# Linear attention and a mixer MLP, gated: tails in two DMAs, the gate vector from GpSimd, an earlier x tile, and four small moves of order

## The chip, the cores and the metric

The kernel runs on one core of a Trainium2 chip. A core has TensorE (PE, with its weight loads shown apart as PEld), VectorE (DVE), ScalarE (ACT), GpSimd (POOL) and SyncE (SP), and 16 DMA engines that move data between HBM and the on-chip memory. The metric is the device time of one execution in microseconds (us). Before the change its median over 3 runs is 1114.06 us (1113.56 to 1114.44).

## The reference

One input x of 2048 tokens by 576 features goes through two blocks, and a gate mixes the results. Everything is float32.

```
g   = sigmoid(sum(x * gate_w))                    # one number per token
# block A: linear attention, 32 heads of 18 features
q, k, v = split(x @ wqkv)
phi(t)  = where(t > 0, t + 1, exp(t)) + 1e-6
kv  = sum over tokens of phi(k) v^T               # 18 x 18 for each head
z   = sum over tokens of phi(k)
o   = (phi(q) kv) / (phi(q) z + 1e-6)
a   = o @ wo
# block B: layer norm, 576 -> 4608, gelu, 4608 -> 576
y   = (x - mean) / sqrt(var + 1e-5)
b   = gelu(y @ w1 + b1) @ w2 + b2
out = g * a + (1 - g) * b
```

## The kernel before, in words

**Tiles.** The tokens stand in 16 tiles of 128. The 576 features of a contraction are four blocks of 128 and a *tail* of 64. A float32 operand is cut into a high part (an fp32r copy made by ACT) and a low part (DVE subtracts the copy from the original), and a product is the sum of high x high, high x low and low x high. For a tail, high and low part share one block: rows 0 to 63 hold the high part, rows 64 to 127 the low one. So the tail of an x tile or of a weight is loaded twice, into both halves of the partitions. `load_twice` (L137) does that in one DMA whose source has an outer dimension of 2 with stride 0:

```
by.dma_start(dst, bass.AP(tensor=src.tensor, offset=src.offset, ap=[[0, 2], [ld, r], [st, n]]))
```

In the trace `t<-in_xm` is the main part of an x tile (256 KB) and `t<-in_xe` its tail (64 KB); `s<-in_wm` and `s<-in_we` are those of a half of the key or query weights (576 and 144 KB); `wv<-in_wve` is the tail of the value weights (288 KB). `y<-t` and `y<-s` are the cuts of an x tile and of a weight, on ACT (copy) and on DVE (subtraction). All helper calls are recorded with line L113, so that groups are told by their tiles.

**Order.** Every engine runs its instructions in the order in which the Python program calls them (the class `InOrder`, L105), so a wait holds all that stands behind it on its engine. All loads and stores are issued by SP, but for four of the first weight, which ACT issues. SP and ACT share eight completion semaphores for their DMAs in rotation: a DMA is issued only when the one eight places ahead of it has landed. The gate vector (`accs<-in_gw`, 2.4 KB) is loaded by two DMAs from SP.

**First stage (L481 to L566).** Three x tiles and four weight halves are loaded and cut. `first_keys(n, half)` is the product of 14 matmuls of x tile n with a half of the key weights; the order list gives pairs of blocks of x and of w, where 0 to 3 are high main blocks, 5 to 8 low main blocks, and 4 and 9 the tails. Between the first and the second product PE turns the gate vector into a column (five transposes), which DVE copies behind the second key half as its column 289, so that the gate's sum comes out of the key product; a column of ones behind it gives the mean.

**Loop over the other 13 tiles (L640 to L662).** Step n computes keys of tile n (28 matmuls), cuts tile n + 1, applies phi, adds the products of tile n - 1 to the sums over tokens (`ps<-ks,xs`), and, but for the last three tiles, computes queries (28 matmuls). Tiles live in a ring of three buffers (`yt`). Beside this, jobs in a table by step (`at(n, f)`) prepare the MLP's input: a *pair* of tiles is loaded (`accs<-in_xm`, `accs<-in_xe`, and its means and scales `accs<-moments`), normalised on DVE (`accs<-accs`), combined and stored as `yd`. `scale_in` and `scale_out` make 1/sqrt(var) of a pair: a power on POOL and one Newton step of four tiny DVE operations; `share_moments` transposes the small table (four DVE transposes) and stores it.

**Attention out (L892 to L906).** In step i of the second loop PE transposes the queries of tile i + 1 (`transpose_q`; ACT and DVE cut the result into `qt`), multiplies tile i's by the values (`attend`, 28 matmuls `ps<-wp,qt`), DVE divides the queries of tile i + 3 by their sums (`normalize`: reduce, add, reciprocal, multiply) and POOL multiplies those of tile i + 4 by the sums (`weigh`).

**MLP (L1163 on).** 18 windows of 14 products each with a seven-product scheme, with jobs in a list sorted by a number `14 * w + x`; `split_w1(k, False)` and `split_w1_rest(k, False)` cut the second part of first-layer weight chunk k into `wb`.

Of the kernel before, what the change touches and what calls it, by code (L numbers as in the profile page):

```python
# [17 lines left out]
P = 128  # L18
S, D, H, DH, F = 2048, 576, 32, 18, 4608
NT = S // P  # L20
HALF = D // 2
# [95 lines left out]
def tile_gated_mix(ctx: ExitStack, tc: tile.TileContext, x, xm, xe, wm, we, wvm, wve, wo, um, ue, w2, b1, b2, gw, out):  # L117
# [19 lines left out]
    def load_twice(dst, src, by=sp):  # L137
        (ld, r), (st, n) = src.ap
        by.dma_start(dst, bass.AP(tensor=src.tensor, offset=src.offset, ap=[[0, 2], [ld, r], [st, n]]))
# [344 lines left out]
    load_w(KEY, 0, ((0, 1), (1, 2), (2, 4), (4, 5)), act)  # L484
    act.activation(tiny, ones[:, 0:1], AF.Exp)
    load_x(first[1])
    sp.dma_start(gwr[:, :D], gw.rearrange("(a n) -> a n", a=1))
    sp.dma_start(gwr[:, D:], gw[4 * P:D].rearrange("(a n) -> a n", a=1))
# [13 lines left out]
    split_w(KEY, 0, pieces=((0, 1), (1, 2)))  # L502
    split_x(first[0], ((4, 5),))
    split_w(KEY, 0, pieces=((2, 4), (4, 5)))

    def first_keys(n, half):
        project(first[n], KEY, half, HI_FIRST, 3 * half + n)
# [10 lines left out]
    first_keys(0, 0)  # L518
# [3 lines left out]
    first_keys(1, 0)  # L522
    split_x(first[2])
    first_keys(2, 0)
    dve.tensor_copy(wraw[KEY, 1][:, :, HALF:HALF + 1], column[:, :, None])
    dve.memset(wraw[KEY, 1][:, :, HALF + 1:HALF + 2], 1.0)
# [113 lines left out]
    for n in range(FIRST, NT):  # L640
        i, before = ORDER[n], ORDER[n - 1]
        if n + 2 < NT:
            load_x(ORDER[n + 2])
        project(i, KEY, 0)
        keys_phi(i, 0)
        project(i, KEY, 1)
        if n + 1 < NT:
            split_x(ORDER[n + 1])
        keys_phi(i, 1)
        moments_of(before)  # L650
        if n + 1 < NT:
            load_xn(ORDER[n + 1])
        keys_split(i)
        add_products(before, 0)
        split_xn(i)
        run(3 * n)
        if n < NT - LATE:
            projected(i, QUERY)
            queries_out(i)
        run(3 * n + 1)  # L660
        add_products(before, 1)
        run(3 * n + 2)  # L662
# [190 lines left out]
    def during(i, f, *args):  # L853
        extra[min(i, NT - 1)].append(lambda: f(*args))
# [25 lines left out]
    during(5, scale_out, NP - 1)  # L880
    during(5, share_moments, NP - 1)
# [10 lines left out]
    for i in range(NT):  # L892
# [7 lines left out]
        if i + 3 < NT:  # L900
            normalize(i + 3)
# [194 lines left out]
    for k in range(HALF_TIME):  # L1096
        w, x = k // 2, 7 * (k % 2)
        if k >= EARLY:
            x1 = x + (0, 0)[k % 2] if k + 1 < HALF_TIME else x - 1
# [151 lines left out]
```

## Time and profile before

| | |
|---|---|
| median of 3 runs | 1114.06 us |
| the profiled execution | 1112.49 us, of it 1110.7 us span |
| PE busy | 1091.2 us (98%) |
| DVE, ACT, POOL busy | 883.5, 571.5, 303.1 us |
| DMA | 206.21 MB, 186 GB/s on the mean |
| granted TensorE clock | 0.998 |

The span is cut by the program into the first stage (to about 47 us), the loop over tiles (to about 197 us), sums and value projection (to about 220 us), attention out (to about 290 us) and the MLP. A matmul's end in the trace is modelled, so a stretch in which PE is "busy" can hide waiting; the number of matmuls in a window tells it. Rows of the timeline give start, duration, engine, operation, tiles written and read, how many instructions were merged, and in brackets the idle time before and what ended it. SPq and ACTq are the issue of DMAs on SP and ACT.

### The profile page before, as it was taken

The page shows a single profiled execution, that of the slowest core. Times are in us where ns is not written, and L with a number is a line of the kernel's source. Part 1 is how long each engine was busy: PE and PEld are TensorE (multiplying, and loading weights), DVE is VectorE, ACT ScalarE, POOL GpSimd, SP SyncE. Part 2 cuts the span into 40 slices and gives each one's busy share as a digit, 9 for nine tenths or more (in the row PEclk, how much of TensorE's full clock was granted, in tenths as well). Part 3 has the DMA queues.
Part 4 walks back from the last instruction along what each step waited for, and adds up shares of the span by engine and source line. Part 5 has one row for each costly group of instructions (what it writes and reads, how often), then busy time and mean ns, then how long its engine had stood idle before and what let it go on. Part 6 is the DMA issues. An engine that isn't in the chain of part 4 may idle for free.

```text
span 1110.7 us, 17958 instructions
## 1 busy us (share of the span) xinstructions
PE 1091.2 (98%) x6657; PEld 997.7 (90%) x6657; DVE 883.5 (80%) x1296; ACT 571.5 (51%) x918; POOL 303.1 (27%) x216
## 2 busy tenths in 40 slices
PE   7999998999999999999999999999999999999998
PEld 7999997999878989889898899989999999999998
DVE  3699988699789999999999996895665656656687
ACT  3767656344566645555555554455444444444450
POOL 0000000672022222312232223333443424324300
PEclk9999999999999999999999999999999999999999
DMA  5385675584974537445465489646534434434342
GB/s 168 110 265 200 219 240 194 188 341 177 320 258 178 191 140 253 158 159 182 172 213 179 144 297 399 202 150 203 149 106 141 149 106 141 146 108 140 106 152 86
DMA packets 126342, 206.21 MB, mean 186 GB/s; under 512 B 9113, under 2 KB 82105, under 8 KB 122288
## 3 DMA queue, kind: packets, MB, share of 16 engines
q1 hardware_dynamic: 125566, 204.34, 54.8%
q8 instruction: 52, 0.85, 0.3%
q10 hardware_dynamic: 690, 0.74, 0.2%
q14 instruction: 34, 0.28, 0.1%
HBM read 135.95 MB, written 69.09 MB: 185 GB/s over the span
## 4 chain that ended last, share of the span: by engine, by line
PE 76%; DVE 12%; DMA 5%; ACT 3%; issue 2%; SPq 1%; ACTq 0%; DVEq 0%
PE ps L113 76%; DVE h L113 2%; DVE accs L113 2%; DMA s<-in_we 2%; DVE wa L113 2%; DVE w_ops L113 1%; DVE qz L113 1%; SPq L113 1%; DMA t<-in_xe 1%; ACT wa L113 1%; DVE u L113 1%; ACT e L113 1%; DMA w_raw<-in_ue 1%; DVE w2r L113 1%; DVE w_raw L113 1%
## 5 line engine op out<-in xcount | busy, mean ns | idle before, releaser
L113 PEld LDWEIGHTS ps<-w_ops,h 128*128 128x128 f32 x2856 | 427.1, 188 | 41.9 <-DVE w_ops L113 2.9
L113 PE MATMUL ps<-w_ops,h 128*128 128x288 f32 x2856 | 452.7, 295 | 1.7 <-ACT accs L113 0.9
L113 PE MATMUL ps<-y,wa 128*128 128x512 f32 x1008 | 277.0, 392 | 0.5 <-DVE wa L113 0.3
L113 POOL TENSOR_TENSOR u<-u 128x512 f32<-128x512 f32 x116 | 176.0, 1542 | 280.7 <-DVE h L113 149.0
L113 DVE TENSOR_TENSOR accs<-ps,accs 128x576 f32<-128x576 f32 x210 | 158.5, 755 | 106.6 <-PE ps L113 99.7
L113 PE MATMUL ps<-y,wb 128*128 128x512 f32 x756 | 202.4, 393 | 0.1
L113 PEld LDWEIGHTS ps<-y,wa 128*128 128x128 f32 x1008 | 174.1, 188 | 20.9 <-DVE wa L113 0.8
L113 ACT ACTIVATE u<-u,b1s 128x512 f32<-128x512 f32 x110 | 79.8, 725 | 215.6 <-DVE u L113 215.6
L113 PE MATMUL ps<-y 128*128 128x288 f32 (+1 forms) x1088 | 157.1, 303 | 9.8 <-ACT y L113 6.1
L113 PEld LDWEIGHTS ps<-y 128*128 128x128 f32 x1088 | 152.5, 194 | 14.0 <-ACT y L113 7.4
L113 DVE TENSOR_TENSOR h<-u,h 128x1024 fp32r<-128x1024 f32 x119 | 157.2, 1321 | 3.5 <-ACT h L113 3.5
L113 PEld LDWEIGHTS ps<-y,wb 128*128 128x128 f32 x756 | 132.4, 188 | 18.7 <-DVE u L113 0.7
L113 ACT ACTIVATE h<-u 128x1024 fp32r<-128x1024 f32 x119 | 125.2, 1053 | 39.0 <-PE ps L113 36.8
L113 POOL TENSOR_TENSOR w2r<-w2r 128x576 f32<-128x576 f32 x48 | 73.0, 1521 | 258.3 <-DVE w2r L113 149.4
L113 ACT ACTIVATE u<-ps 128x512 f32<-128x512 f32 x110 | 65.1, 594 | 101.7 <-PE ps L113 101.6
L113 DVE TENSOR_TENSOR u<-ps,u 128x512 f32<-128x512 f32 x110 | 75.4, 686 | 36.4 <-PE ps L113 23.4
L113 DVE TENSOR_TENSOR w_ops<-w2r,w_ops 128x576 fp32r<-128x576 f32 x119 | 98.1, 825 | 0.0
L113 ACT ACTIVATE w_ops<-w2r 128x576 fp32r<-128x576 f32 x119 | 79.7, 670 | 0.5 <-DMA w2r<-in_w 0.5
L113 PE MATMUL ps<-wp,qt 128*128 128x288 f32 x448 | 63.3, 297 | 2.0 <-DVE qt L113 2.0
L113 PEld LDWEIGHTS ps<-wp,qt 128*128 128x128 f32 x448 | 59.9, 188 | 2.3 <-DVE qt L113 2.3
L113 DVE TENSOR_TENSOR accs<-accs 128x384 f32<-128x384 f32 (+3 forms) x67 | 58.4, 881 | 2.3 <-DMA accs<-moments 0.8
L113 DVE TENSOR_TENSOR w_raw<-w_raw 128x384 f32<-128x384 f32 x64 | 53.8, 841 | 1.6 <-DMA w_raw<-in_ue 0.8
(139 smaller groups left out, 843.0 us busy)
## 6 DMA issues: line engine op xcount, KB each, us to landing
wa<-w1d SPq DMA_DIRECT2D x80, 320.0 KB
w2r<-in_w SPq DMA_DIRECT2D x72, 288.0 KB
w1d<-wa SPq DMA_DIRECT2D x16, 1280.0 KB
wb<-w1d SPq DMA_DIRECT2D x60, 320.0 KB
y<-yd SPq DMA_DIRECT2D x14, 1280.0 KB
w1d<-wb SPq DMA_DIRECT2D x16, 960.0 KB
w_raw<-in_um SPq DMA_DIRECT2D x96, 128.0 KB
yd<-ys SPq DMA_DIRECT2D x15, 640.0 KB
```

What stands on the lines that cost most here:

```text
L113: return lambda *args, **kwargs: self.tc.keep_in_program_order(op(*args, **kwargs))
```

## The change

Seven edits; the arithmetic stays the same, but for the order in which the first product is summed.

- `load_twice` issues two DMAs of 64 partitions each, both from the same source, where it issued one of 128. It is called for 16 x tiles, four weight halves and the value weights: 21 more DMAs.
- The two DMAs of the gate vector are issued by GpSimd (ahead of its mask) and no longer by SP.
- ACT issues the tail of the first key half behind its table load and the `tiny` activation, and no longer ahead of them.
- The first product's order is the high and low blocks 0 and 1, then 2 and 3, then the products with the weight's low part, and the two with the tails last. ACT and DVE cut weight blocks 2 and 3 ahead of the x tile's tail.
- The column of the gate vector is copied ahead of the cut of the third x tile.
- From step FIRST on, the load in the loop is for tile n + 3 and stands behind the cut of tile n + 1; it was for n + 2 at the head of the step. In the first of these steps both are issued.
- The Newton step and the transposes of the last pair stand inside `normalize` of attention step 5, ahead of its multiply; they stood at the end of the step. The cut of `wb` for chunk 2 stands half a place later.

```diff
     def load_twice(dst, src, by=sp):
-        (ld, r), (st, n) = src.ap
-        by.dma_start(dst, bass.AP(tensor=src.tensor, offset=src.offset, ap=[[0, 2], [ld, r], [st, n]]))
+        for half in range(2):
+            by.dma_start(dst[half * 64:(half + 1) * 64], src)
...
     load_x(first[0])
-    load_w(KEY, 0, ((0, 1), (1, 2), (2, 4), (4, 5)), act)
+    load_w(KEY, 0, ((0, 1), (1, 2), (2, 4)), act)
     act.activation(tiny, ones[:, 0:1], AF.Exp)
+    load_w(KEY, 0, ((4, 5),), act)
+    pool.dma_start(gwr[:, :D], gw.rearrange("(a n) -> a n", a=1))
+    pool.dma_start(gwr[:, D:], gw[4 * P:D].rearrange("(a n) -> a n", a=1))
     load_x(first[1])
-    sp.dma_start(gwr[:, :D], gw.rearrange("(a n) -> a n", a=1))
-    sp.dma_start(gwr[:, D:], gw[4 * P:D].rearrange("(a n) -> a n", a=1))
     load_x(first[2])
...
     split_x(first[0], ((0, 4),))
-    split_w(KEY, 0, pieces=((0, 1), (1, 2)))
+    split_w(KEY, 0, pieces=((0, 1), (1, 2), (2, 4)))
     split_x(first[0], ((4, 5),))
-    split_w(KEY, 0, pieces=((2, 4), (4, 5)))
-
-    def first_keys(n, half):
-        project(first[n], KEY, half, HI_FIRST, 3 * half + n)
+    split_w(KEY, 0, pieces=((4, 5),))
+
+    def first_keys(n, half, order=HI_FIRST):
+        project(first[n], KEY, half, order, 3 * half + n)
...
-    first_keys(0, 0)
+    first_keys(0, 0, HH[:2] + LH[:2] + HH[2:] + LH[2:] + HL + TAIL)
     split_x(first[1])
...
     first_keys(1, 0)
+    dve.tensor_copy(wraw[KEY, 1][:, :, HALF:HALF + 1], column[:, :, None])
+    dve.memset(wraw[KEY, 1][:, :, HALF + 1:HALF + 2], 1.0)
     split_x(first[2])
     first_keys(2, 0)
-    dve.tensor_copy(wraw[KEY, 1][:, :, HALF:HALF + 1], column[:, :, None])
-    dve.memset(wraw[KEY, 1][:, :, HALF + 1:HALF + 2], 1.0)
...
     for n in range(FIRST, NT):
         i, before = ORDER[n], ORDER[n - 1]
-        if n + 2 < NT:
+        if n == FIRST:
             load_x(ORDER[n + 2])
...
         if n + 1 < NT:
             split_x(ORDER[n + 1])
+        if n + 3 < NT:
+            load_x(ORDER[n + 3])
         keys_phi(i, 1)
...
-    during(5, scale_out, NP - 1)
-    during(5, share_moments, NP - 1)
...
         if i + 3 < NT:
-            normalize(i + 3)
+            normalize(i + 3, (0,))
+            if i == 5:
+                scale_out(NP - 1)
+                share_moments(NP - 1)
+            normalize(i + 3, (1,))
...
-            x1 = x + (0, 0)[k % 2] if k + 1 < HALF_TIME else x - 1
+            x1 = x + 0.5 * (k == EARLY) if k + 1 < HALF_TIME else x - 1
```

Three places show what the table of instructions makes of it. The first is ACT at the start of the program; `s` is the first key half, `t` the first x tile, `y` their cuts:

```order
 L113 DMA s<-in_wm 128x288 x2
 L113 DMA s<-in_wm 128x2x288
-L113 DMA s<-in_we 128x1x288
 L113 ACT_TABLE_LOAD
 L113 ACTIVATE tiny<-ones 128x1
+L113 DMA s<-in_we 64x288 x2
 L113 ACTIVATE y<-t 128x512
 L113 ACTIVATE y<-s 128x288 x2
+L113 ACTIVATE y<-s 128x576
 L113 ACTIVATE y<-t 128x128
-L113 ACTIVATE y<-s 128x576
 L113 ACTIVATE y<-s 128x288
```

The tail's DMA went behind the table load and became two; the cut of weight blocks 2 and 3 (`128x576`) went ahead of that of the x tail.

The second is SP in steps 12 and 13 of the tile loop, first as it was (`yd` are stores of prepared pairs, `xn` the x tile in its other layout):

```order
L113 DMA t<-in_xm 128x512
L113 DMA t<-in_xe 128x1x128
L113 DMA xn<-in_x 128x576
L113 DMA accs<-in_xm 128x2x256
L113 DMA accs<-in_xe 128x1x128 x2
L113 DMA accs<-in_xm 128x2x256
L113 DMA accs<-in_xe 128x1x128 x2
L113 DMA accs<-moments_107 128x512
L113 DMA yd_131<-ys_545 128x2x640
L113 DMA t<-in_xm 128x512
L113 DMA t<-in_xe 128x1x128
L113 DMA xn<-in_x 128x576
```

and now:

```order
L113 DMA t<-in_xm 128x512
L113 DMA t<-in_xe 64x128 x2
L113 DMA xn<-in_x 128x576
L113 DMA accs<-in_xm 128x2x256
L113 DMA accs<-in_xe 128x1x128 x2
L113 DMA accs<-in_xm 128x2x256
L113 DMA accs<-in_xe 128x1x128 x2
L113 DMA accs<-moments_107 128x512
L113 DMA yd_131<-ys_554 128x2x640
L113 DMA xn<-in_x 128x576
```

The x tile stands at the same place of SP's queue, but it is the last of the 16 where it was the last but one, and the place behind the pair's loads, where the last tile stood, is empty.

The third is DVE in attention step 5 (`qz` are the sums of queries, `mt`, `mr` and `mrt` the moments), before:

```order
L113 RECIPROCAL qz<-qz 128x32
L113 SCALAR_TENSOR_TENSOR acc_right<-acc_right,qz 128x576
L113 TENSOR_TENSOR mt<-mr 128x2
L113 TENSOR_TENSOR mt<-mt 128x2
L113 TENSOR_SCALAR mt<-mt 128x2
L113 TENSOR_TENSOR mr<-mr,mt 128x2
L113 STREAM_TRANSPOSE mrt<-mr 32x32 x4
L113 TENSOR_TENSOR qt<-ps,qt 128x512
```

and now:

```order
L113 RECIPROCAL qz<-qz 128x32
L113 TENSOR_TENSOR mt<-mr 128x2
L113 TENSOR_TENSOR mt<-mt 128x2
L113 TENSOR_SCALAR mt<-mt 128x2
L113 TENSOR_TENSOR mr<-mr,mt 128x2
L113 STREAM_TRANSPOSE mrt<-mr 32x32 x4
L113 SCALAR_TENSOR_TENSOR acc_right<-acc_right,qz 128x576
L113 TENSOR_TENSOR qt<-ps,qt 128x512
```

The eight small operations went ahead of the multiply that ends `normalize`.

## The prediction

> **What bounds the kernel now.** I read the shares of the engines first, then PE's waits, then the timeline and the counts of matmuls in short windows around each wait.
>
> ```profile
> PE 1091.2 (98%) x6657; PEld 997.7 (90%) x6657; DVE 883.5 (80%) x1296; ACT 571.5 (51%) x918; POOL 303.1 (27%) x216
> ...
> PE ps L113 <- ACT y L113: 6.1, 4, 3.4
> PE ps L113 <- DVE k L113: 3.4, 1, 3.4
> PE ps L113 <- DVE qt L113: 2.0, 1, 2.0
> ```
>
> PE sets the end. What an edit is worth is the time by which PE gets earlier to work it then does without a gap. Its three named waits lie where the change works: the cuts `y` of the start (four waits), phi of the keys near the loop's end, `qt` in the attention.
>
> The start first, by the timeline of PE, ACT and ACT's queue:
>
> ```profile
> 2.22 1.12 ACTq L113 DMA_DIRECT2D s<-in_we  x1
> 4.77 0.61 ACT L113 ACTIVATE y<-t 128x512 fp32r<-128x512 f32 x1
> 5.29 0.76 ACT L113 ACTIVATE y<-s 128x288 fp32r<-128x288 f32 x2
> 5.77 0.94 PE L113 MATMUL ps<-y 128*128 128x288 f32 x2 [0.45 <-ACT y L113]
> 7.29 0.31 ACT L113 ACTIVATE y<-t 128x128 fp32r<-128x128 f32 x1 [1.23 <-DMA t<-in_xe]
> 7.50 0.67 ACT L113 ACTIVATE y<-s 128x576 fp32r<-128x576 f32 x1
> 8.22 1.81 PE L113 MATMUL ps<-y 128*128 128x288 f32 x6 [1.51 <-ACT y L113]
> 12.92 0.44 ACT L113 ACTIVATE y<-s 128x288 fp32r<-128x288 f32 x1 [4.75 <-DMA s<-in_we]
> 13.41 2.06 PE L113 MATMUL ps<-y 128*128 128x288 f32 x6 [3.38 <-ACT y L113]
> 16.03 17.32 PE L113 MATMUL ps<-y 128*128 128x288 f32 x112
> 37.69 3.88 PE L113 MATMUL ps<-y 128*128 128x288 f32 x28
> ```
>
> The first product's 14 matmuls end only at 15.47 us (13.41 + 2.06), since the tail of the first weight half, issued at 2.22, lands at 12.92. Windows of 1 us (busy PE and matmuls, granted clock, share of the DMA engines, GB/s) show why:
>
> ```profile
> 3.00:4.00 1.00, 1.00 (x6) 1.00 1.00 356
> 8.00:9.00 1.00, 0.78 (x3) 1.00 0.14 46
> 16.00:17.00 1.00, 1.00 (x5) 1.00 1.03 366
> 22.00:23.00 1.00, 1.00 (x10) 1.00 0.39 131
> ```
>
> Main parts move at 356 GB/s over all 16 engines. When only tails are left (8 to 9) it is 46 GB/s at a share of 0.14, which is two engines of 16 (0.125), and two is the outer dimension of a tail's source. At 46 GB/s a weight tail of 144 KB takes 3.1 us, and four tails stand before 12.9 us. The trace shows this rate wherever the tails are alone.
>
> The end of the tile loop:
>
> ```profile
> 144.28 0.46 SPq L113 DMA_DIRECT2D t<-in_xm  x1
> 156.17 0.67 SPq L113 DMA_DIRECT2D t<-in_xe  x1
> 160.21 3.90 PE L113 MATMUL ps<-y 128*128 128x288 f32 x28
> 167.78 0.74 ACT L113 ACTIVATE y<-t 128x640 fp32r<-128x640 f32 x1 [4.61 <-DMA t<-in_xe]
> 168.54 1.01 DVE L113 TENSOR_TENSOR y<-t,y 128x512 fp32r<-128x512 f32 x2 [4.89 <-ACT y L113]
> 168.56 4.00 PE L113 MATMUL ps<-y 128*128 128x288 f32 x28 [0.71 <-ACT y L113]
> 168.74 0.76 SPq L113 DMA_DIRECT2D accs<-moments  x1
> 173.83 1.95 DVE L113 TENSOR_TENSOR accs<-accs 128x768 f32<-128x768 f32 x2 [0.76 <-DMA accs<-moments]
> 177.75 0.74 ACT L113 ACTIVATE y<-t 128x640 fp32r<-128x640 f32 x1 [5.13 <-DMA t<-in_xe]
> 179.13 0.46 DVE L113 SCALAR_TENSOR_TENSOR k<-ps,e 128x288 f32<-128x288 f32 x1
> 179.73 5.51 PE L113 MATMUL ps<-y 128*128 128x288 f32 x28 [3.42 <-DVE k L113]
> 188.83 3.88 PE L113 MATMUL ps<-y 128*128 128x288 f32 x28
> 196.28 1.13 PE L113 MATMUL ps<-pks,ones 128*128 128x288 f32 x4
> ```
>
> ACT waits 4.61 us for the tail of the last tile but one, 11.6 us after its issue at 156.17; phi stands behind the wait, DVE idles 4.89 and comes late to phi of the next keys (179.13), and PE waits 3.42 for the bank that this frees and then takes 5.51 instead of 3.90 for 28 matmuls.
>
> **The change, part by part.** The profiled execution took 1112.49 us (1.79 outside its span), 1.57 below the median of 1114.06; the sum is made against it and 1.57 is put back.
>
> *The start.* With halves of 64 partitions the source's outer dimension is 64, so I take the rate of the main parts. ACT now issues both halves ahead of its first cut. By the eight shared semaphores these issues wait for the first x tile's main part (landed by 4.77) and for half of its tail, which follows it; the cut moves from 4.77 to about 5.4. Then ACT runs 0.61 + 0.76 + 0.67 + 0.31 + 0.44 = 2.8 us of cuts, to 8.2, if the tail has landed by 7.8, 2.4 us after its issue; the first weight pieces, issued ahead of the tail at 2.22, are in use at 5.29, with all engines full in between. DVE's last cut follows in 0.5, the two tail matmuls end at 9.2, five transposes take the 0.56 that lie between 15.47 and 16.03 now, and the second product starts at 9.8 instead of 16.03.
>
> From there PE needs 21.66 us to the 28 matmuls at 37.69. Of these the first five run at 5 a microsecond, the rest at 10 (windows at 16 and 22). The slow part can shrink, since PE has been working from 5.8 on, or come back whole. A cut that is late would show here next: the second key half, which PE needs after two more products, at about 13.5. I put SP's issue of it at 6 to 7 (eight DMAs in flight, the first landed by 4.77), and its 720 KB at 356 GB/s are 2 us. So PE's 21.66 us stay and the gain is 16.03 - 9.8 = 6.2; with the 0 to 1.7 us of the slow part I take **6.5**. Bounds: 8.2 above; below, if the halves land 2.5 us later than I put them, 3.7.
>
> The Trainium skill (*TensorE: Matmul & The Clock Gate*, Part 1) says that the PE clock is halved until about 3.4 us of sustained work have passed and again after an idle window. The counts of 5 and 10 agree with half and full rate, though the clock column says 1.00 in both. By that rule alone the slow part comes back whole and this term is 6.2.
>
> A rule of the Trainium skill speaks against the edit: *DMA: Bandwidth & Descriptors*, section "Rules for kernel authors", says of two transfers to disjoint partition halves "Don't bother — they serialize", because both use the same 16 engines. The row of 46 GB/s says that the DMA replaced is not on 16 engines; the same page's section on how many engines a DMA uses (the largest number up to 16 that divides both outer dimensions) gives 2 for it and 16 for a half, and that agrees with 0.14. By the first rule this term would be below nothing (the second rival).
>
> *21 more DMAs* cost SP their issue; in the row of `t` a tail's issue is 0.55 us at the median.
>
> ```profile
> L113 SPq DMA_DIRECT2D t<-in_xe x16: 523/550/887, 1.3 to 170.5; - x16
> ```
>
> In the loop that is at most 0.55 a step, and a step is about 11 us (the loads at 144 and 155 to 156 are a step apart). What waits behind it is `xn`, used a step later: nothing.
>
> *The gate vector from GpSimd.* No DMA of GpSimd is in this trace. PE needs the vector at 9.2; POOL issues it behind a few memsets. Below it costs nothing; above there is no row, so it is the third rival.
>
> *The x tile a step ahead.* The place that now brings the last tile is the one behind 155 us; the one at 144.28 brings the last but one. That tile then has 19 us to ACT's need at 163.2 (167.78 - 4.61), against the 11.6 that its slow tail took: the waits of 4.61 and 5.13 go, whatever the halves are worth. Without any wait, PE's blocks of 7.64 us (160.21 to 167.85, where the gap of 0.71 begins) follow each other: three of them and the last of 7.45 (188.83 to 196.28) are 30.4 against 36.07 from 160.21 to 196.28, so 5.7 at most. What is late next is DVE: its phi at 179.13 moves up by 4.89, and by 0.76 more if the pair's `moments` (issued 168.74, used 173.83) land 5 us earlier. SP's place for that pair is unchanged, and it must wait until DVE has read the buffer of the pair before, which I put at 161 to 162 from where DVE stands before its idle 4.89; then 168.74 becomes about 164 to 165, if the queue is no longer held up by the value weights' tail of 288 KB (6.3 us at 46 GB/s). Phi then ends at 174 to 175 and PE wants it at 175.5. I take **5.0**; bounds 1 (moments as late as now) and 5.7.
>
> *Newton steps.* DVE, POOL and PE in the attention:
>
> ```profile
> 249.57 0.76 DVE L113 SCALAR_TENSOR_TENSOR acc_right<-acc_right,qz 128x576 f32<-128x576 f32 x1
> 250.44 1.41 DVE L113 TENSOR_TENSOR mt<-mt 128x2 f32<-128x2 f32 x1
> 253.15 1.02 DVE L113 TENSOR_TENSOR qt<-ps,qt 128x512 fp32r<-128x512 f32 x2
> 254.22 2.91 PE L113 MATMUL ps<-wp,qt 128*128 128x288 f32 x20 [2.02 <-DVE qt L113]
> 257.44 3.96 PE L113 MATMUL ps<-wp,qt 128*128 128x288 f32 x28
> ```
>
> A multiply of two numbers took 1.41 us beside POOL's `weigh`, which starts when the multiply at 249.57 has ended. The eight operations fill 250.33 to 253.15; with the long one at 0.2 they are 1.6. Ahead of the multiply they make it end at 251.95, PE's transposes of the next tile come 1.6 later than now, at 252.0, and `qt` at 252.0 instead of 253.15. The attention block that ends at 257.1 starts at 252.6 and needs 3.96: 256.5. I take **0.6**, bounds 0 (another DVE operation is stretched beside `weigh`) and 1.0.
>
> *First order, column, `wb`.* The first order is in the 9.2 already. In window 1 only DVE's order changes:
>
> ```profile
> 322.35 1.55 DVE L113 TENSOR_TENSOR wb<-w_raw,wb 128x768 fp32r<-128x768 f32 x2
> 323.92 0.56 DVE L113 TENSOR_TENSOR w_raw<-w_raw 128x384 f32<-128x384 f32 x1
> ```
>
> These two swap; what follows starts when both are done. `wb` is used at 328.8, 4 us later. Nothing, at most 0.3 either way.
>
> Sum: 6.5 + 5.0 + 0.6 = 12.1; 1112.49 - 12.1 + 1.57 = **1102.0 us**.
>
> **The rivals.**
>
> *The loop's end keeps its wait* (12%). The `moments` land as late as now because the pair's load waits for DVE, not for the queue. For it: that load cannot start before 162. Against it: DVE's own 4.89 us go. The term is 1 instead of 5: 1106.
>
> *The halves are no faster* (9%): the rate of 46 GB/s has another reason than the outer dimension. Then ACT's early wait costs 0.6 to 1 at the start, the loop's term stays (it does not need the halves) at 3 to 5: 1109. Against it stands 356 against 46 GB/s, 16 to 2.
>
> *The gate vector comes late* (5%), the case of the other side. PE's transposes stand in order behind the first product. If the vector lands at T, PE is held from 9.2 to T and each microsecond costs one. From 21.3 (9.2 + 12.1) on the kernel is slower than before; at 25, 1117.7. For it: nothing in the trace prices a DMA of GpSimd. Against it: 2.4 KB have some 7 us.
>
> *More comes free* (9%): the tails also sat on the two engines through the loop and delayed stores; with the whole slow part and 1 to 2 us of DVE's waits in the loop, 1098.
>
> **How the numbers follow.** The forecast has 65%. Its own range is 1112.49 + 1.57 - (8.2 + 5.7 + 1.0) = 1099 to, with 4.5 + 3 + 0.2, 1106. With the rivals above and below, 8 in 10 lie in 1097.5 to 1108. About 0.2% (2.2 us) can be told from no change. The gate vector gives slower 3% and no change 1%; mishaps of several terms at once add 3% to no change and 1% to slower. Faster: 92%.
>
> **What would show it.** Right: the cut of the first weight's tail near 8 us, the 112 matmuls starting at 9.5 to 10.5, no stretch of 46 GB/s in the first 30 us; no wait of ACT for `t<-in_xe` behind 150; the gap of 3.42 gone and its 28 matmuls back at 3.9; the mt multiply at 0.2. Wrong: a PE wait ahead of the five transposes (gate vector), SP standing on semaphores in the start, a wait of DVE for `moments`, or PE's gain at 37.69 given back where DVE is at its fullest (60 to 105 us).

## The result and the profile after

The changed kernel takes **1099.37 us** (median of 4 runs, 1098.53 to 1101.21), the kernel before 1113.81 (4 runs beside it, 1113.44 to 1114.44). The ratio is 0.9872, with a 95% interval of 0.9855 to 0.9889: 1.3% faster, 14.4 us. The forecast was 1102.0 and its range 1097.5 to 1108.0. The profiled execution took 1099.95 us (span 1098.0), 12.54 less than the one of before.

PE's share, and its longest waits, as the page and the list of waits of the changed kernel have them (total us, times, longest us):

```profile
PE 1086.0 (99%) x6657; PEld 993.8 (91%) x6657; DVE 882.7 (80%) x1296; ACT 571.6 (52%) x918; POOL 305.3 (28%) x218
...
PE ps L113 <- DVE acc_right L113: 1.7, 1, 1.7
PE ps L113 <- ACT y L113: 1.3, 2, 1.0
PE ps L113 <- DVE k L113: 1.2, 2, 0.7
```

The waits of 6.1 for `y` and 3.4 for `k` are 1.3 and 1.2 now; the one for `qt` is gone and one of 1.7 for `acc_right` is new.

Where the time came from is read at three places that PE reaches in both kernels in the same order: the 28 matmuls that stood at 37.69 (I call it the landmark), the product of ones by `pks` at the loop's end, and the first product of the MLP.

| PE reaches | before | after | gained so far | gained in this stretch |
|---|---|---|---|---|
| landmark | 37.69 | 30.13 | 7.56 | start 7.56 (forecast 6.5) |
| ones by `pks` | 196.28 | 184.26 | 12.02 | loop 4.46 (5.0) |
| first MLP product | 290.49 | 277.64 | 12.85 | attention 0.83 (0.6) |
| end of the span | 1110.7 | 1098.0 | 12.7 | rest -0.15 (0) |

The start of the changed kernel, by the timeline of ACT's queue, ACT and PE (start, us, engine, operation; in brackets the idle time before and what ended it):

```profile
4.11 1.21 ACTq L113 DMA_DIRECT2D s<-in_we  x2
5.37 0.63 ACT L113 ACTIVATE y<-t 128x512 fp32r<-128x512 f32 x1 [1.64 <-DMA t<-in_xe]
6.38 3.60 PE L113 MATMUL ps<-y 128*128 128x288 f32 x14 [1.04 <-ACT y L113]
8.16 0.45 ACT L113 ACTIVATE y<-s 128x288 fp32r<-128x288 f32 x1 [0.60 <-DMA s<-in_we]
10.31 3.99 PE L113 MATMUL ps<-y 128*128 128x288 f32 x28
13.04 1.42 ACT L113 ACTIVATE y<-s 128x1450 fp32r<-128x1450 f32 x1 [2.98 <-DMA s<-in_we]
14.51 1.48 PE L113 MATMUL ps<-y 128*128 128x290 f32 x9 [0.21 <-ACT y L113]
```

In the kernel before, the second key half was cut here:

```profile
19.86 1.42 ACT L113 ACTIVATE y<-s 128x1450 fp32r<-128x1450 f32 x1 [3.92 <-DMA s<-in_we]
```

The tail of the first weight half is issued at 4.11 and cut at 8.16 (12.92 before). The second product starts at 10.31 (16.03). The second key half, a whole weight of main part and tail, is cut at 13.04 instead of 19.86. PE stands 0.21 us for this cut, and 0.23 us for its low part on DVE.

The loop's end and the attention (timeline of SP, DVE and PE):

```profile
157.07 0.47 SPq L113 DMA_DIRECT2D accs<-moments  x1
162.55 1.95 DVE L113 TENSOR_TENSOR accs<-accs 128x768 f32<-128x768 f32 x2 [1.37 <-DMA accs<-moments]
168.45 3.97 PE L113 MATMUL ps<-y 128*128 128x288 f32 x28 [0.72 <-DVE k L113]
176.65 3.98 PE L113 MATMUL ps<-y 128*128 128x288 f32 x28 [0.49 <-DVE k L113]
237.55 0.16 DVE L113 TENSOR_TENSOR mt<-mt 128x2 f32<-128x2 f32 x1
239.82 0.66 PE L113 MATMUL ps<-accs,acc_right 128*128 128x128 f32 x4 [1.71 <-DVE acc_right L113]
```

PE's gap of 3.42 and its block of 5.51 are now a gap of 0.49 and a block of 3.98. The block was long because PE ran at half its clock behind the gap: in before the granted clock is 0.50 in each window of 1 us from 181 to 184. All that the loop gains lies at its end: from the landmark to PE's block at 160.21 (152.61 now) it is 122.5 us in both kernels. `moments` is issued at 157.07 instead of 168.74: 11.7 us earlier, 7.6 of it by the start. The long multiply of the Newton steps takes 0.16 instead of 1.41, and PE's wait there is 1.71 instead of 2.02 + 0.23.

So the sum came out, in part by luck: the terms are off by +1.06, -0.54 and +0.23, the rest of the span by -0.15. Whether the terms belong to the edits they were booked under is for the experiments.

### The profile page after: what moved, and what is told of

Same layout as the page of the kernel before. It is cut to its first block, busy times and chain, and to the rows that moved or that the text cites. A ratio compares the mean times of both kernels' runs of the same rounds, so it can differ in the third digit from the quotient of the medians.

```text
span 1098.0 us, 17985 instructions
## 1 busy us (share of the span) xinstructions
PE 1086.0 (99%) x6657; PEld 993.8 (91%) x6657; DVE 882.7 (80%) x1296; ACT 571.6 (52%) x918; POOL 305.3 (28%) x218
## 4 chain that ended last, share of the span: by engine, by line
PE 76%; DVE 12%; DMA 5%; ACT 3%; issue 2%; SPq 2%; ACTq 0%; DVEq 0%
PE ps L113 76%; DVE h L113 2%; DVE accs L113 2%; SPq L113 2%; DVE wa L113 2%; DVE w_ops L113 1%; DMA t<-in_xm 1%; DVE u L113 1%; ACT wa L113 1%; DMA w_raw<-in_ue 1%; ACT e L113 1%; DMA b2b<-in_b 1%; DVE w2r L113 1%; DVE w_raw L113 1%; DMA w2r<-in_w 1%
## 5 line engine op out<-in xcount | busy, mean ns | idle before, releaser
L113 PE MATMUL ps<-y 128*128 128x288 f32 (+1 forms) x1088 | 152.8, 298 | 3.0 <-ACT y L113 1.3
L113 PEld LDWEIGHTS ps<-y 128*128 128x128 f32 x1088 | 148.8, 190 | 6.7 <-ACT y L113 1.8
```

What stands on the lines that cost most here:

```text
L113: return lambda *args, **kwargs: self.tc.keep_in_program_order(op(*args, **kwargs))
```

## The experiments

The edits are shown against the changed kernel or against the kernel before, as named. Medians stand beside the kernel before on the same chip: 1114.12, 1113.98 and 1113.48 for the three groups of runs, in the order below.

**The halves alone**, on the kernel before:

```
 def load_twice(dst, src, by=sp):
-    (ld, r), (st, n) = src.ap
-    by.dma_start(dst, bass.AP(..., ap=[[0, 2], [ld, r], [st, n]]))
+    for half in range(2):
+        by.dma_start(dst[half * 64:(half + 1) * 64], src)
```

> The kernel before with only the tails loaded by two DMAs, each from a plain source of 64 rows. My theory (a tail was slow because a source with outer dimension 2 is moved by two engines, and each place that waited for a tail waited for that): the start gains about 7, as in the changed kernel, so the 28 matmuls that stood at 37.69 us start at 30 to 31; and because the tile's tail issued behind 155 us now lands after some 3 us instead of 11.6, ACT's waits of 4.61 and 5.13 in the loop's end go too, without the look-ahead, so the product of ones by pks starts at 184 to 186 (196.28 before, 184.26 changed); the time is 1100 to 1102. The rival (the look-ahead carries the loop's end, as the prediction's sum has it): the start gains the same, but the loop's end keeps 3 to 4.4 of its waits, the product starts at 187.5 to 189, the time is 1103 to 1105.

Measured: 1101.99 us (1101.25 to 1103.5), ratio 0.9893 (0.9878 to 0.9908). The start, the loop's end and the attention, from ACT, DVE and PE:

```profile
13.36 1.42 ACT L113 ACTIVATE y<-s 128x1450 fp32r<-128x1450 f32 x1 [2.54 <-DMA s<-in_we]
30.66 3.89 PE L113 MATMUL ps<-y 128*128 128x288 f32 x28
163.09 1.95 DVE L113 TENSOR_TENSOR accs<-accs 128x768 f32<-128x768 f32 x2 [1.34 <-issue]
165.75 0.74 ACT L113 ACTIVATE y<-t 128x640 fp32r<-128x640 f32 x1 [2.14 <-DMA t<-in_xe]
184.77 1.13 PE L113 MATMUL ps<-pks,ones 128*128 128x288 f32 x4
242.69 4.45 PE L113 MATMUL ps<-wp,qt 128*128 128x288 f32 x20 [2.00 <-DVE qt L113]
```

The second key half is cut 6.5 us earlier than before (13.36), the landmark is 7.03 earlier. From the landmark to ones by `pks` it is 184.77 - 30.66 = 154.11 us, against 158.59 before and 154.13 with the whole change. ACT still waits 2.14 for a tile, but DVE's pair work starts at 163.09 all the same, and PE does not feel the wait. The halves alone bring the start and the whole of the loop's end; of the 14.4 us they bring 12.1. The forecast had the loop's end "whatever the halves are worth", by the look-ahead. (The row of 4.45 is taken up with the Newton steps.)

**Everything but the halves**: the changed kernel with `load_twice` as it was (the same diff backwards).

> The changed kernel with its tails in one DMA again (outer dimension 2). My theory: the start's term goes, since the tail is slow again: the 112 or so matmuls of the second product start at 14 to 16 us instead of 10.31, the landmark of 28 matmuls is back at 36 to 38 (30.13 changed); the loop's end keeps most of its 4.4, since the look-ahead asks for the tile a step earlier; the time is 1105 to 1107. The rival (the look-ahead does nothing without quick tails, since more slow tails queue on the same two engines): the loop's end is as before, and the time is 1110 to 1112.

Measured: 1112.51 us (10 runs, 1111.7 to 1113.81), ratio 0.9988 (0.9979 to 0.9997). ACT, SP, DVE and PE:

```profile
14.89 0.44 ACT L113 ACTIVATE y<-s 128x288 fp32r<-128x288 f32 x1 [7.13 <-DMA s<-in_we]
19.62 1.41 ACT L113 ACTIVATE y<-s 128x1450 fp32r<-128x1450 f32 x1 [3.03 <-DMA s<-in_we]
156.15 5.45 SPq L113 DMA_DIRECT2D xn<-in_x  x1
168.07 0.80 SPq L113 DMA_DIRECT2D accs<-moments  x1
171.13 0.73 ACT L113 ACTIVATE y<-t 128x640 fp32r<-128x640 f32 x1
173.25 1.95 DVE L113 TENSOR_TENSOR accs<-accs 128x768 f32<-128x768 f32 x2 [3.15 <-DMA accs<-moments]
179.15 6.44 PE L113 MATMUL ps<-y 128*128 128x288 f32 x28 [3.25 <-DVE k L113]
```

The start is lost, and the loop's end too: 196.63 - 37.55 = 159.08 us. The look-ahead does here what it says: ACT cuts the tile at 171.13 without a wait. But SP still stands 5.45 us at `xn`, as in before:

```profile
156.94 5.49 SPq L113 DMA_DIRECT2D xn<-in_x  x1
```

`moments` is issued at 168.07 (168.74) and DVE waits 3.15 for it instead of 0.76. The wait has moved from `t` to `moments` and PE's gap stays, 3.25 against 3.42. This is the outcome of the prediction's first rival (the `moments` land as late as now), and it comes true just where the halves are missing, but not for the rival's reason: SP's queue is held, the pair's load does not wait for DVE. Where the tails are halves, SP does wait for DVE ahead of that load (5.4 us, to 153.31, in the changed kernel), and the load is in time all the same.

**Two DMAs of outer dimension 2**: the changed kernel with each tail in two DMAs again, but cut by columns.

```
-    for half in range(2):
-        by.dma_start(dst[half * 64:(half + 1) * 64], src)
+    (ld, r), (st, n) = src.ap; c = n // 2
+    for half in range(2):
+        by.dma_start(dst[:, half * c:(half + 1) * c],
+                     bass.AP(..., offset=src.offset + half * c * st, ap=[[0, 2], [ld, r], [st, c]]))
```

> The changed kernel with each tail in two DMAs, but cut by columns, so that each of the two still has a source of outer dimension 2. As many transfers and bytes as in the changed kernel. My theory (outer dimension sets the number of engines): slow as with one DMA, the stretches where only tails move stay near 46 GB/s if both DMAs sit on the same two engines, at most twice that if not; the landmark of 28 matmuls is at 34 to 38 and the time 1103 to 1107. The rival (two transfers in flight are what makes it fast): as the changed kernel, landmark at 30.1, time 1099 to 1100.

Measured: 1118.21 us (6 runs, 1116.99 to 1119.18), ratio 1.0036 (1.0023 to 1.0049): slower than before. Windows of 1 us (PE, PEld, DVE, ACT, POOL busy; granted clock; share of the DMA engines; GB/s) and PE:

```profile
7.00:8.00 1.00, 0.00 (x0) 0.00 (x0) 0.28 (x1) 0.94 (x3) 0.00 (x0) 1.00 0.13 45
12.00:13.00 1.00, 0.00 (x0) 0.00 (x0) 0.00 (x0) 0.00 (x0) 0.00 (x0) 1.00 0.14 45
185.98 6.05 PE L113 MATMUL ps<-y 128*128 128x288 f32 x28 [4.99 <-DVE k L113]
```

As many transfers as in the changed kernel, and still 45 GB/s at a share of 0.13 to 0.14: both DMAs sit on the same two engines. What counts is the source's outer dimension, not that there are two transfers. My own time of 1103 to 1107 was missed as well: with 21 more slow DMAs SP stands longer (3.73 us at the two tails of a tile at 164.25), and PE's gap in the loop is 4.99. Whether that comes from the further issues or from the shorter rows is not separated.

The kept traces also have the times at which each DMA raised its completion semaphore. A transfer on all 16 engines raises it 16 times as its data land; I read one such increment as one engine, which for two of them agrees with the share of 0.14:

| DMA, outer dimension of its source | issued | increments when its data land | the last two of them |
|---|---|---|---|
| before, `t<-in_xm`, 128 | 155.29 | 16; 14 of them by 158.97 | 165.61, 166.11 |
| before, `t<-in_xe`, 2 | 156.17 | 2 | 167.24, 167.75 |
| before, `wv<-in_wve`, 2 | 149.72 | 2 | 164.47, 164.89 |
| before, `accs<-in_xe` (`four_times`), 4 | 163.17 | 4 | 169.54, 169.99 |
| columns, `s<-in_we`, 2 | 4.16 | 2 | 10.06, 10.10 |
| columns, the other half of its columns, 2 | 6.49 | 2 | 13.36, 13.37 |
| changed, a half of `t<-in_xe`, 64 | 146.04 | 16 | 152.60, 153.25 |

(Where there are fewer than 16, one more entry at the end of the issue stands for the others.) The count follows the outer dimension, 2, 4 or 16, and not the number of transfers or the repeated read: the loads by `four_times` read their source four times with stride 0 and have 4, and `accs<-moments`, 128 times with stride 0, has 16. The two late increments of the main part come just behind those of the value weights' tail, and those of the tile's tail behind both. So the slow tails also held back two of the 16 parts of the transfers issued behind them, and the tail that ACT waited for at 167.78 had stood behind the value weights' tail.

**Without the look-ahead**: the changed kernel with the loads of the x tiles at their old place.

```
-        if n == FIRST:
+        if n + 2 < NT:
             load_x(ORDER[n + 2])
...
-        if n + 3 < NT:
-            load_x(ORDER[n + 3])
```

> The changed kernel with the load of each x tile back at the head of the step two ahead of its use. My theory (quick tails alone cure the loop's end): no change beyond 0.7 us against the changed kernel, the product of ones by pks starts at 184 to 185.5, no wait of ACT for t<-in_xe of over 1 us behind 150 us. The rival (the look-ahead carries the loop's end): 3 to 4.4 us are lost, the product starts at 187 to 189, time 1103.

Measured: 1098.49 us (1098.41 to 1100.37), ratio 0.9864 (0.9849 to 0.9879). ACT, DVE and PE:

```profile
161.31 1.95 DVE L113 TENSOR_TENSOR accs<-accs 128x768 f32<-128x768 f32 x2 [1.03 <-DMA accs<-moments]
164.06 0.75 ACT L113 ACTIVATE y<-t 128x640 fp32r<-128x640 f32 x1 [1.91 <-DMA t<-in_xe]
183.00 1.13 PE L113 MATMUL ps<-pks,ones 128*128 128x288 f32 x4
```

Landmark 29.22, so 153.78 us to ones by `pks`, against 154.13 with the look-ahead. ACT's wait of 1.91 is back and costs nothing, since DVE behind it waits for `moments` in the same time. In these runs the look-ahead is worth nothing with quick tails, and without them (everything but the halves) nothing either.

**Newton steps behind the block**, on the changed kernel:

```
+    during(5, scale_out, NP - 1)
+    during(5, share_moments, NP - 1)
...
-            normalize(i + 3, (0,))
-            if i == 5:
-                scale_out(NP - 1)
-                share_moments(NP - 1)
-            normalize(i + 3, (1,))
+            normalize(i + 3)
```

> The changed kernel with the last Newton steps back behind the attention block in which they stood. My theory (the move is worth 0.8: from the product of ones by pks to the first product of the MLP the kernel before took 290.49 - 196.28 = 94.21 us, the changed one 277.64 - 184.26 = 93.38): this stretch is 94.0 to 94.4 again, PE waits some 2 us for qt once instead of 1.71 for acc_right, the time is 0.8 above the changed kernel's, 1099.5 to 1101. The rival (the stretch is shorter for another reason, such as where the x tiles' loads stand): it stays at 93.3 to 93.5.

Measured: 1102.05 us (1098.47 to 1102.34), ratio 0.9889 (0.9873 to 0.9905). PE, and one window of 1 us behind the gap:

```profile
242.18 4.44 PE L113 MATMUL ps<-wp,qt 128*128 128x288 f32 x20 [2.02 <-DVE qt L113]
243.00:244.00 1.00, 1.00 (x6) 1.00 (x5) 0.93 (x3) 0.00 (x0) 0.00 (x0) 0.50 0.07 23
```

From ones by `pks` to the first MLP product it is 279.97 - 184.31 = 95.66 us, not the 94.21 of before, which I had expected back. The same wait of 2.02 for `qt` is there, but the 20 matmuls behind it take 4.44 us and not 2.91: the granted clock is 0.60, 0.50, 0.50 and 0.70 in the four windows from 242 to 246, which is 3.4 us at the half. The stretch in all the runs sorts them:

| kernels | from ones by `pks` to the MLP |
|---|---|
| Newton steps inside: changed, one DMA, columns, no look-ahead, gate vector on SP, old first order, rows first | 93.38, 93.32, 93.33, 93.33, 93.40, 93.32, 93.32 |
| outside, full clock behind the gap: before, 22 unread matmuls | 94.21, 94.14 |
| outside, half clock behind it: halves alone, this one, 8 unread matmuls | 95.73, 95.66, 95.73 |

(Newton late and both steps together, further down, have 93.31 and 93.23.) So the move is worth 0.8 us in the one case and 2.3 in the other, because a gap of 2.0 us may or may not cost PE its clock, and the 1.62 to 1.71 that are left did not in any of these profiles. The same kernel may well have both cases: of the four runs with the steps outside one took 1098.47 us (clock 0.999), the others 1101.83 to 1102.34 (0.995 to 0.998); only one of the longer ones was profiled. Of the two expectations, mine was right in direction and too small. In the profiles the 2.3 are also what the halves alone lacked, 95.73 against 93.38 in this stretch; the medians, 1101.99 and 1099.37, agree with it, though the intervals of their ratios overlap.

**The gate vector on SP**, on the changed kernel:

```
-    pool.dma_start(gwr[:, :D], ...)
-    pool.dma_start(gwr[:, D:], ...)
     load_x(first[1])
+    sp.dma_start(gwr[:, :D], ...)
+    sp.dma_start(gwr[:, D:], ...)
```

> The changed kernel with the gate vector's two DMAs issued by SP again, behind the second x tile's. My theory (they only take SP's time, some 1.2 us, so x tiles and the second key half are asked for later): the landmark of 28 matmuls moves from 30.13 to 30 to 31.3, by later cuts of the second key half, no PE wait ahead of the five transposes; time 0 to 1.2 above the changed kernel's. The rival (on SP the vector comes late, because SP stands behind eight transfers in flight): a PE wait of 1 to 4 us ahead of the five transposes, time 1 to 4 above.

Measured: 1098.51 us (1098.43 to 1099.31), ratio 0.9866 (0.9851 to 0.9881). No PE wait ahead of the five transposes; the second product starts at 10.71, the landmark is at 30.02. Who issues the vector makes no difference; it is late on neither queue.

**The old first order**, on the changed kernel:

```
-    load_w(KEY, 0, ((0, 1), (1, 2), (2, 4)), act)
+    load_w(KEY, 0, ((0, 1), (1, 2), (2, 4), (4, 5)), act)
     act.activation(tiny, ones[:, 0:1], AF.Exp)
-    load_w(KEY, 0, ((4, 5),), act)
...
-    split_w(KEY, 0, pieces=((0, 1), (1, 2), (2, 4)))
+    split_w(KEY, 0, pieces=((0, 1), (1, 2)))
     split_x(first[0], ((4, 5),))
-    split_w(KEY, 0, pieces=((4, 5),))
+    split_w(KEY, 0, pieces=((2, 4), (4, 5)))
...
-    first_keys(0, 0, HH[:2] + LH[:2] + HH[2:] + LH[2:] + HL + TAIL)
+    first_keys(0, 0)
```

> The changed kernel with the first product's order of terms, ACT's order of cuts and the place of the weight tail's issue (ahead of ACT's table load) as before. My theory (the tail's data is there at about 8, and the old order wants it at the ninth matmul, 8.4 to 9): ACT issues the tail some 2 us earlier and runs its first cut up to 1 us later, as in the kernel before with halves alone, where the first cut stood at 6.40 and the second product at 11.82; so the second product starts at 10.5 to 12 instead of 10.31, the landmark stands at 30.2 to 31, the time is 0 to 1.2 above the changed kernel's. The rival (the order does nothing, as the prediction had it, plus or minus 0.3): second product at 10.0 to 10.6.

Measured: 1099.79 us (1098.55 to 1101.49), ratio 0.9877 (0.9861 to 0.9894). PE's second and third product:

```profile
11.79 15.24 PE L113 MATMUL ps<-y 128*128 128x288 f32 x112
30.62 3.88 PE L113 MATMUL ps<-y 128*128 128x288 f32 x28
```

The second product starts 1.48 us later than in the changed kernel (10.31), as expected, yet the landmark is only 0.49 later (30.13), and the runs overlap. Two thirds of what the order gains at 10 us is given back at the second key half, where the changed kernel waits and this one does not. In the other runs with the new first order and quick tails the landmark stands at 29.09 (both steps, further down) to 30.16, so at the landmark the order is worth 0.5 to 1.5 us; the medians do not show it.

**PE kept busy in the gap of the first product**, on the kernel before. Unread matmuls of ones by ones stand between the eighth and the ninth matmul; 22 in the first run, 8 in the second:

```
+        if m == 8:
+            for _ in range(22):
+                pe.matmul(ps[:, 7, :P], ones, ones, start=True, stop=True)
```

> The kernel before with 22 matmuls of ones by ones, whose result nobody reads, put into PE's order between the eighth and the ninth matmul of the first product, where PE otherwise waits 3.38 us for the tail's cut. Theory of the clock (PE ran at half its rate from 13.4 to about 21 us because it had stood idle before): with PE busy in the gap, the six matmuls behind it take about 1.0 instead of 2.06 us, the first of the 112 start about 15 instead of 16.03, they run at 10 a microsecond from the start, and the landmark is 2 to 2.7 us ahead of 37.69, at 35.0 to 35.7. The rival (the rate is low for another reason, such as transfers that fill the memory at the same time: 356 to 366 GB/s at 16 us): six matmuls in 2 us, landmark at 37.3 to 38.

Measured: one run, 1113.98 us. PE (each unread matmul has two records), and a window:

```profile
9.82 7.23 PE L113 MATMUL ps<-ones 128*128 128x128 f32 x44
16.81 1.05 PE L113 MATMUL ps<-y 128*128 128x288 f32 x6
18.18 15.24 PE L113 MATMUL ps<-y 128*128 128x288 f32 x112
11.00:12.00 1.00, 1.00 (x7) 1.00 (x7) 0.00 (x0) 0.00 (x0) 0.00 (x0) 0.50 1.07 359
```

The clock half of the expectation holds: the six matmuls take 1.05 instead of 2.06 us, the 112 take 15.24 instead of 17.32. The other half fails, since the 22 ran at half the clock and held PE to 16.81; so the second product starts 2.15 later, and the landmark comes at 37.80, as before. Hence the second run, with 8 of them.

> The kernel before with 8 unread matmuls in the gap of the first product, not 22, since the 22 held PE until 16.81: they ran at half rate to 14. Theory of the clock (some 4 to 6 us of unbroken work bring the full rate, an idle stretch takes it away): the eight fill PE from 9.82 to about 13.2, the six matmuls behind the gap start at 13.2 to 13.5 and take 1.1 to 1.9, the 112 start at 15 to 15.7 and take 15.2 to 16 instead of 17.32, the landmark is at 35 to 36.2 instead of 37.69. The rival (the second weight half is late, cut at 19.86, so that PE cannot be earlier behind it): the 112 start early, but break with a wait of 1 to 2 us at about 20, landmark at 37 to 37.7.

Measured: one run, 1112.78 us. PE and ACT:

```profile
13.46 1.42 PE L113 MATMUL ps<-y 128*128 128x288 f32 x6 [0.98 <-ACT y L113]
15.21 3.99 PE L113 MATMUL ps<-y 128*128 128x288 f32 x28
19.99 1.41 ACT L113 ACTIVATE y<-s 128x1450 fp32r<-128x1450 f32 x1 [3.89 <-DMA s<-in_we]
21.45 13.02 PE L113 MATMUL ps<-y 128*128 128x290 f32 x84 [2.25 <-ACT y L113]
```

The rival holds. The first 28 of the 112 are done 2 us earlier and at the full rate, and then PE waits 2.25 us for the second key half, whose cut stays where it was (19.99; 19.86 in before). The landmark is at 38.07, no earlier than in before. In the kernel before the slow PE of 16 to 21 us cost nothing: it reached the second key half when that was ready. What held the start was this second half, and the first tail with it.

**Two further steps on the changed kernel.** The first puts the last Newton steps behind the eighth attention block:

```
-            if i == 5:
-                scale_out(NP - 1)
-                share_moments(NP - 1)
...
+    during(7, scale_out, NP - 1)
+    during(7, share_moments, NP - 1)
```

> The changed kernel with the last Newton steps (and the transposes and the small store behind them) moved out of the sixth attention block to behind the eighth, two blocks later, in which DVE cuts no pair. My theory (PE's wait of 1.71 us for acc_right is the 1.6 us of these operations put ahead of the multiply, since DVE also cuts 2.0 us of wb in that block): the wait falls to 0 to 0.2 and comes up nowhere else; from the product of ones by pks to the first product of the MLP 91.6 to 92.0 us instead of 93.38; time 1.5 below the changed kernel's, 1097 to 1098. The rival (DVE is full all through the attention, 0.94 of each microsecond at 236 to 243, so the 1.6 us come out later): a wait of 1 to 1.7 in one of the blocks behind, 93.0 to 93.6 us.

Measured: 1098.30 us (1097.64 to 1099.54), ratio 0.9870 (0.9855 to 0.9885). PE, POOL and DVE:

```profile
237.70 0.66 PE L113 MATMUL ps<-accs,acc_right 128*128 128x128 f32 x4 [0.23 <-DVE acc_right L113]
244.21 1.43 POOL L113 TENSOR_TENSOR qz<-acc_right,pks 128x576 f32<-128x576 f32 x1 [1.80 <-DVE mt L113]
244.24 1.42 DVE L113 TENSOR_TENSOR mt<-mt 128x2 f32<-128x2 f32 x1
246.28 0.60 PE L113 MATMUL ps<-accs,acc_right 128*128 128x128 f32 x4
251.22 0.66 PE L113 MATMUL ps<-accs,acc_right 128*128 128x128 f32 x4 [0.28 <-DVE acc_right L113]
255.81 0.66 PE L113 MATMUL ps<-accs,acc_right 128*128 128x128 f32 x4
260.38 0.66 PE L113 MATMUL ps<-accs,acc_right 128*128 128x128 f32 x4
```

My theory falls. The wait of 1.71 is 0.23, but the stretch is 276.93 - 183.62 = 93.31 us, as with the steps inside. The transposes that follow each other every 4.25 us elsewhere come 4.94, 4.59 and 4.57 apart from 246.28 on: 1.35 us in three blocks, mostly below what the list of waits shows. DVE has no room there (17.14 of the 18 us from 244 to 262), and the long multiply is 1.42 again: it starts just behind POOL's `weigh` and ends with it. The 1.26 that this adds to DVE's sum is about what is given back. The same move with the multiply clear of `weigh` was not tried.

The second asks for a pair's rows of moments ahead of its tiles:

```
 def load_pair(sup, j):
-    load_raws(sup, j)
     load_rows(sup, j)
+    load_raws(sup, j)
```

> The changed kernel with the rows of moments of a pair asked for ahead of its x tiles instead of behind them. My theory (DVE's wait of 1.37 us for accs<-moments at 162.55, and PE's two waits of 0.72 and 0.49 for k behind it, come from the moments being last in SP's queue): the first operation of the pair starts about 161.2, PE's two waits are 0 to 0.3, the time from the landmark of 28 matmuls (30.13) to the product of ones by pks falls from 154.13 to 152.9 to 153.5; time 0.6 to 1.2 below. The rival (the x tiles' tails in four copies are then last and DVE waits for these): a wait of DVE for accs<-in_xe or in_xm of 0.8 to 1.5 at the same place, 153.8 to 154.3.

Measured: 1098.11 us (1096.88 to 1099.3), ratio 0.9867 (0.9851 to 0.9883). DVE and PE:

```profile
160.74 1.95 DVE L113 TENSOR_TENSOR accs<-accs 128x768 f32<-128x768 f32 x2
182.44 1.13 PE L113 MATMUL ps<-pks,ones 128*128 128x288 f32 x4
```

DVE does not wait, PE's two waits for `k` are gone, and from the landmark (29.79) it is 152.65 us, 1.48 below the changed kernel. The moments' landing was the last wait of the loop's end, as the prediction had named it.

Both together:

> The changed kernel with both: the last Newton steps two blocks later and the rows of moments first. If the two theories hold they add: 2.2 to 2.8 below the changed kernel, 1095.7 to 1097.2. By the rivals: as the changed kernel, 1098.5 to 1100.

Measured: 1097.39 us (4 runs, 1096.95 to 1098.17), ratio 0.9863 (0.9846 to 0.9880). From the landmark (29.09) to ones by `pks` (181.70) 152.61, then 93.23 to the MLP: the gain is that of the rows alone. It is the lowest of all medians, 2 us below the changed kernel, but the two ratios' intervals overlap; what the trace shows for certain is the 1.5 us at the loop's end.

## Why the prediction was right, point by point

**The time** is 2.6 us below the forecast. 0.4 is the sum (12.54 against 12.1). The other 2.2 is the 1.57 that I put back because the profile of before lay below its median, and 0.58 by which the profile of after lies above its own.

**The rate of the tails** was read rightly: 46 GB/s at a share of 0.14 means two engines, and two is the source's outer dimension. The run with columns shows that it is not the number of transfers, since two transfers of outer dimension 2 stay at 45 GB/s and 0.13 to 0.14; the counts of 2, 4 and 16 increments show that it is the dimension. Of the four tails that the prediction had before 12.9 us, three had landed by 13.09 and the fourth at 15.13: the two engines also had their shares of the main parts to move. The Trainium skill (*DMA: Bandwidth & Descriptors*, section "Why a DMA increments its semaphore by 16 and not by 1") has the largest number up to 16 that divides the outer dimensions; these runs agree. The Trainium skill's rule that halves serialize, in "Rules for kernel authors", is about two transfers that have all 16 engines each, and does not hold for a source that had two. The second rival (halves no faster) is out by the halves alone.

**The start**: 6.5 forecast, 7.56 measured. The first cut was put at 5.4 (5.37), the tail's cut at about 8 (8.16), the second product at 9.8 (10.31). The step that failed is "From there PE needs 21.66 us": it took 19.82. I had left the slow part of PE as 0 to 1.7 of gain in itself. The runs with unread matmuls show that without the tails' rate this part is worth nothing, because the second key half comes when it comes. Two waits lay side by side, and the halves moved both. With the whole change the second product starts 5.7 us earlier and the second half is cut 6.8 earlier (19.86 to 13.04); with the halves alone it is 4.2 (11.82) and 6.5 us, and the landmark follows the second half. Of the 1.84 us, 0.6 lie behind the first stage, from PE's first `ps<-xs,ks` to the landmark (4.36 us before, 3.75 now); why is not shown. I had named the second half as what is late next, put PE's need at 13.5 and its data in time; it was 0.21 late.

**The loop's end**: 5.0 forecast, 4.46 measured: the size is right by luck, under the wrong name. The step that failed is "the waits of 4.61 and 5.13 go, whatever the halves are worth" and with it the second rival's "the loop's term stays (it does not need the halves)". By the runs it is all the halves' and none the look-ahead's. The wait of ACT that I took for the cause was one of two; the other was SP standing at `xn` and issuing `moments` late. I had written that condition down ("if the queue is no longer held up by the value weights' tail") and 164 to 165 for the issue, which is 157.07 + 7.6. I did not see that the condition alone decides. The tile's tail stood behind the value weights' tail, by the increments; what of SP's stand at `xn` comes from which tail is not settled.

**Newton steps**: 0.6 forecast, 0.83 measured, for the reason given: the long multiply became 0.16. That PE's clock behind the gap could make it 2.3 was not in the forecast. The later end of the `acc_right` multiply, which I had put 1.6 us behind its old one, is the new wait of 1.71.

**First order, gate vector, more DMAs**: nothing, as forecast, in the time. The order's 1.48 us at 10 us shrink to 0.49 at the landmark (up to 1.5 against other runs). The third rival (gate vector late) is out: no PE wait ahead of the transposes with either issuer. No cost of the 21 more DMAs shows as long as each is quick; with slow ones of the same number the kernel is slower than before. The fourth rival (more comes free) came half true: the start gained more than its 6.5, but the loop up to its end gained nothing.

**The sums.** The upper bound of the start should be 6.2 + 1.7 = 7.9; 8.2 counts part of the slow stretch twice. The upper end of the forecast's own range, 1106, uses 4.5, 3 and 0.2 and not the lower bounds given with the terms; with 3.7, 1 and 0 it is 1109. The second rival's 1109 takes its loop term at the full 5; with 3 it is 1111.

**Wrong in what would show it**: a wait of DVE for `moments` was listed among the signs against the forecast. It is there with 1.37 us, and it is what the loop's end still lost until the rows were asked for first.

## What to carry to other kernels

Look at a transfer's rate when nothing else moves: a share of the DMA engines near c/16 (here 0.14, c = 2) is a reason to look whether its source has an outer dimension of c. Cutting it into transfers with a large outer dimension was worth more here (12.1 of 14.4 us) than all the ordering of work around it. Where a wait is to be removed, look for a second one that ends at the same time, behind the same consumer; an edit can take the one that the trace names and leave the time as it is. On an engine that is full over a stretch, ask what an edit takes from the sum of its work there; where the operation stands may change only the name of the wait.

## What was not expected of the hardware

A gap of PE of 2.0 us, at the same place of the same program part, left the granted clock at full in two kernels (20 matmuls in 2.91 and 2.92 us) and halved it in three (4.44 to 4.45 us, 1.5 us lost). The Trainium skill (*TensorE: Matmul & The Clock Gate*, Part 1) says that the activity window is free-running and about 3.4 us long; that agrees with a gap of 2.0 us which sometimes counts and sometimes does not, and with the 3.4 us at the half clock behind it in the run with the Newton steps outside. The Trainium skill also has, in the same Part, the clock fall after at least one idle window of about 3.4 us; here a gap of 2.0 us, less than one, was enough.

In the kernel before, PE ran five to six matmuls a microsecond at 16 to 20 us with 1.00 in the clock column; with the Newton steps outside the column says 0.50 for six of the same matmuls (243 to 244 us). In the kept trace of before, the record of the granted clock has its first entry at 20.51 us, with 1.00; the column shows 1.00 ahead of it too. The counts are the safer sign there.

One multiply of DVE on 128 x 2 numbers took 0.16 or 1.41 us by where it stood. It is 1.41 to 1.42 in before and with the Newton steps late; there it starts 0.03 us behind POOL's `weigh` (250.41 in before) and ends within 0.03 us of it. It is 0.16 in the changed kernel, where `weigh` starts 2.3 us later. So by these times it stood until `weigh` was done; this agrees with the Trainium skill (*SBUF — State Buffer*, section "SBUF: two separate sides"): a DVE operation with two inputs in SBUF and one of GpSimd take one pair of ports in turn, and the later of them waits out the whole of the other.
